# Another order for a planned top-k attention and Mixer: three-piece output products, new priorities, earlier release of score buffers

## The chip, the cores and the metric

The kernel runs on one core of one Trainium2 chip. The metric is the device time of one execution in microseconds (us), as the median of several runs; three runs of the kernel before gave 1004.16, 1005.12 and 1007.36 us.

## What is computed

For 8 batches and 8 heads, with 576 positions and a head dimension of 64: scores are formed, only the 32 largest of each row are kept, and their softmax weights the values. The heads are joined to x (576 x 512 for each batch), and a Mixer block follows, first over tokens, then over channels.

```python
scores = scale * np.matmul(q, k.transpose(0, 1, 3, 2))
kth = np.partition(scores, -top_k, axis=-1)[..., -top_k:-top_k + 1]      # top_k = 32
scores = np.where(scores >= kth, scores, -1000000000.0)
attn = np.exp(scores - np.max(scores, axis=-1, keepdims=True))
attn = attn / (np.sum(attn, axis=-1, keepdims=True) + 1e-09)
x = np.matmul(attn, v)                     # heads joined: (8, 576, 512)
...
h = np.maximum(x.transpose(0, 2, 1) @ w_tok1, 0.0) @ w_tok2    # 576 -> 256 -> 576
u = x + h.transpose(0, 2, 1)
out = u + np.maximum(u @ w_ch1, 0.0) @ w_ch2                   # 512 -> 1536 -> 512
```

## The kernel before

**Units.** The work is cut into 32 units, each two heads of one batch; four units make a batch, and each batch ends in a Mixer. A unit's score rows are nine tiles of 128 rows: eight whole ones (four row blocks of two heads) and one made of both heads' last 64 rows. Tiles 0 to 3 are the unit's first half (group 0), tiles 4 to 8 the second (group 1).

**The stages of a half unit, and their engines.**

- TensorE transposes q and k (`qk_tr`), ScalarE copies the result out of PSUM (`qk_ev`). TensorE makes the scores (`s1_mm`, `s0_mm` at line 334, `st_mm`), ScalarE copies them into the score buffer SS (`s1_ev`, `s0_ev` at line 344, `st_ev`).
- VectorE selects: `upper` (line 384), `split4` (lines 407 and 411), four `top_round`s (lines 423 and 426), `low_round` (line 432), which needs `both_bits` and `lower_bits` of GpSimd (lines 390 and 399), and `combine` (lines 438 to 443), which writes the thresholds `kthall`. GpSimd keeps four numbers of each row (`keep_ends`, line 449), from which the end of the program sees whether the fast selection was sound.
- For five tiles of a unit (0, 1, 2, 4, 5) GpSimd scales the thresholds (`raise_kth`, line 496, tile `kbig`), ScalarE makes a steep ramp (`steep`, line 502), GpSimd subtracts it from the scores (`sink`, line 510), ScalarE takes the exponential into `pb` (`expo`, line 483), and SyncE starts a DMA that transposes it into PT (`turn`). For the other four, ScalarE makes E (`expo`) and a mask U (`below_act`, line 526), and TensorE transposes both in one accumulation (`p_tr`, `ptail_tr`, lines 532 and 535), which ScalarE copies into PT (`p_ev`, line 555, and `ptail_ev`).
- TensorE multiplies PT with the values (`o_mm`, line 601, one call for each head), VectorE takes reciprocals (`o_den`, line 613), ScalarE scales into Xb (`o_ev`, line 624).

**The Mixer.** After each unit `h1_mm` and `ut_mm` do the token part for 128 channels. After a batch's fourth unit `h2_mm` (line 689; 12 blocks, each in two parts) and `out_mm` (lines 711 to 719) do the channel part. One `out_mm` is 15 products into one PSUM bank: x by an identity matrix, two of the token part, twelve of the channel part; there are five in a batch, one for each row block. The last batch has a path of its own (`plan_mlp_last`).

**What sets the order.** Nothing runs in the order in which it is written. Every step is a task with an engine, a planned duration, a priority (smaller goes first), predecessors, and the buffers that it takes (`acq`) and frees (`rel`). `Plan.order` plays this through: when an engine is free, the ready task with the smallest priority whose buffers are free is next. The result is the order in which instructions stand on each engine; each engine then works strictly in that order and waits where an input is not there. A wrong planned duration costs nothing by itself, but it puts an instruction where it has to wait. For unit u the priorities are U = 100u plus an offset; for batch b's Mixer M = 400(b + 1) plus an offset. The PSUM banks are tp (two), s0 (three, scores), O (one) and mps (two, Mixer); SS has four buffers, two units' worth.

Two rules of the plan matter below. Sinks and `keep_ends` of a half are held until `lower_bits` of the next half is done (`hold`, `later`). And where TensorE has been idle in the plan, `spare` (line 244) puts fillers in: products whose result nobody reads.

At the end of a half a task of no duration on GpSimd frees its buffers, once the last readers and `keep_ends` are done:

```python
add("POOL", 0.0, U - 1000, lambda: None, deps=done + [keep[g]],
    rel=[("SS", u, g), ("A", u, g), ("nmax", u, g)] + ([("St", u)] if g else [])
    + ([] if fast else [("kbig", u, g)]))
```

Of the kernel before, what the change touches and what calls it, by code (L numbers as in the profile page):

```python
# [11 lines left out]
LAG = {"PE": 0.11, "ACT": 0.15, "DVE": 0.12, "POOL": 0.06, "SP": 1.2, "DQ": 0.0, "SPQ": 0.0}  # L12
# [3 lines left out]
SPARE = 0.8  # L16
SPARE_US = 0.22
# [7 lines left out]
class Plan:  # L25
# [23 lines left out]
    def order(self):  # L49
# [10 lines left out]
        while left:  # L60
# [13 lines left out]
            for e in free:  # L74
# [14 lines left out]
                if best is not None:  # L89
                    ready[e].remove(best)  # L90
                    if e == "PE" and best.dur > 0.0:
                        at, r, i = min(
# [4 lines left out]
                        )  # L97
# [30 lines left out]
def kernel(  # L128
# [11 lines left out]
    nc = tc.nc  # L140
# [565 lines left out]
    def out_mm(mst, sc):  # L706
        Xb, H1T, H2T = mst["Xb"], mst["H1T"], mst["H2T"]
        ss = csz(sc)
        ss_ = slice(sc * P, sc * P + ss)
        ps = bank("mps")  # L710
        nc.tensor.matmul(
            out=ps[0:ss, 0:C], lhsT=identB[0:ss, 0:ss], rhs=Xb[0:ss, sc, :], start=True, stop=False
        )
        for jc in range(NJ):
            nc.tensor.matmul(
                out=ps[0:ss, 0:C], lhsT=w2b[:, jc, ss_], rhs=H1T[:, jc, :], start=False, stop=False
            )
        for fc in range(NF):
            nc.tensor.matmul(  # L719
                out=ps[0:ss, 0:C],  # L720
                lhsT=H2T[:, fc, ss_],
                rhs=wc2b[:, fc, :],
                start=False,
                stop=(fc == NF - 1),
            )
        mst["po", sc] = ps
# [91 lines left out]
    def plan_unit(u):  # L818
# [5 lines left out]
        for name, src in (("q", q), ("k", k), ("v", v)):  # L824
            ld[name] = add("SP", 1.75, U - 230, lambda name=name, src=src: load_one(st, name, src, b, p),
                           acq=[("ld" + name, u)])
        vc = add("POOL", 1.2, U - 50, lambda: vcast(st), deps=[ld["v"]], acq=[("vb", u)],
                 rel=[("ldv", u)], slack=1.3)
        ev, prev = [], None
        for i in range(2):  # L830
            a = add("PE", 0.61, U - 160, lambda i=i: qk_tr(st, i), deps=[ld["qk"[i]], prev], acq=[("tp", u, "q", i)] + ([] if i else [("qkT", u)]), slack=1.3)
            prev = a
            ev.append(
                add("ACT", 0.49, U - 150, lambda i=i: qk_ev(st, i), deps=[a] + ev[-1:],
                    rel=[("tp", u, "q", i)])
            )
        a = add("PE", 0.29, U - 160, lambda: qk_tail_tr(st), deps=[prev], acq=[("tp", u, "t")])
        add("PE", 0.0, U - 160, lambda: None, deps=[a], rel=[("ldq", u), ("ldk", u)])
        ev.append(
            add("ACT", 0.17, U - 150, lambda: qk_tail_ev(st), deps=[a] + ev, rel=[("tp", u, "t")])  # L840
# [6 lines left out]
        for g in range(2):  # L847
            a = add("PE", 0.65, U - 140 + 10 * g, lambda g=g: s1_mm(st, g), deps=ev + smm[-1:],
# [3 lines left out]
            for hh in range(2):  # L852
                evs.append(
                    add("ACT", 0.17, U - 130 + 10 * g, lambda g=g, hh=hh: s1_ev(st, g, hh), deps=[a] + evs,
# [3 lines left out]
            for t in (2 * g, 2 * g + 1):  # L858
                a = add("PE", 1.1, U - 140 + 10 * g + 1, lambda t=t: s0_mm(st, t), deps=[smm[-1]],
                        acq=[("s0", u, t, 0), ("s0", u, t, 1)])  # L860
                smm.append(a)
                for hh in range(2):
                    evs.append(
                        add("ACT", 0.495, U - 130 + 10 * g + 1, lambda t=t, hh=hh: s0_ev(st, t, hh),
                            deps=[a, e0], rel=[("s0", u, t, hh)])
                    )
            if g == 1:
                for part in range(2):
                    a = add("PE", (1.01, 0.28)[part], U - 129, lambda part=part: st_mm(st, part),
# [4 lines left out]
                        add("ACT", (0.49, 0.12)[part], U - 119, lambda part=part: st_ev(st, part),  # L874
# [5 lines left out]
            x = add("DVE", (2.33, 3.19)[g], U + 5 * g, lambda g=g: split4(st, g), deps=[x, chain.get("low")])  # L880
# [16 lines left out]
            x = add("DVE", (1.33, 1.13)[g], U + 5 * g, lambda g=g: combine(st, g, u), deps=[x])  # L897
            keep_ = add("POOL", 0.25, U + 5, lambda g=g: keep_ends(st, g, u), deps=[x])
# [3 lines left out]
            for i in gtiles(g):  # L902
                if i not in st["turned"]:
                    y = add("ACT", 0.68, U - 50 + i, lambda i=i: expo(st, i), deps=[nm, preE] + evs, acq=[("E", u, i)])
                    selE[i] = preE = y
# [282 lines left out]
```

## Time and profile before

| | us |
|---|---|
| median of three runs | 1005.12 |
| profiled execution, its own time | 1006.08 |
| its span, first to last instruction | 1004.2 |
| TensorE busy (fillers included) | 935.5 |
| VectorE busy | 894.6 |
| ScalarE busy | 853.5 |
| GpSimd busy | 727.9 |
| mean granted TensorE clock, of full speed | 0.979 |

The profile is of one execution. An engine's busy time is the time in which at least one of its instructions runs; what it waits for is in a view of its own. In the timeline a row is one instruction or several alike, with start and length, and in brackets the idle time ahead of it and what ended it. In rows of groups stand count, busy time, mean length of one in ns, and idle time ahead. PE is TensorE, DVE VectorE, ACT ScalarE, POOL GpSimd, SPq the DMA queue of SyncE.

### The profile page before, as it was taken

The numbers are of one execution on the slowest core, as the hardware profiler recorded it, in microseconds if no ns is written. First come the engines' busy times: TensorE is split into PE (matmuls) and PEld (weight loads), VectorE is DVE, ScalarE is ACT, GpSimd is POOL, SyncE is SP. The second block draws the span as 40 slices with busy tenths as digits, with TensorE's granted clock in tenths as the row PEclk, the third lists the DMA queues.
The fourth block names the chain that finished last, engine by engine and source line by source line (L and its number), as shares of the span: only waits on it lengthen the run. The fifth ranks groups of instructions, "written<-read, shape, count | busy, mean of one in ns | idle before, by whom it ended". The sixth has DMA issues, their size and how long they took to land. (4 is left out here: it accounts for less than half of the span.)

```text
span 1004.2 us, 22286 instructions
## 1 busy us (share of the span) xinstructions
PE 935.5 (93%) x7128; PEld 502.9 (50%) x7128; DVE 894.6 (89%) x4088; ACT 853.5 (85%) x1976; POOL 727.9 (72%) x598
## 2 busy tenths in 40 slices
PE   9889999899999999999999999899999999989995
PEld 6444444455555455454545455454545555444542
DVE  3999999997999979999799979999799997999801
ACT  5667898898999988998999989999899989999731
POOL 3888888886688858888598867888688885888400
PEclk9989899999999999999999999999999999999998
DMA  7454122133332233123322333232233333211201
GB/s 167 120 174 130 38 63 60 45 63 105 68 69 51 69 87 87 40 62 77 81 58 60 80 100 79 45 68 74 66 69 63 75 99 68 46 34 31 71 1 51
DMA packets 229741, 72.65 MB, mean 72 GB/s; under 512 B 222128, under 2 KB 222704, under 8 KB 229616
## 3 DMA queue, kind: packets, MB, share of 16 engines
q1 hardware_dynamic: 229616, 71.15, 29.8%
q8 instruction: 58, 0.95, 0.4%
q14 instruction: 67, 0.55, 0.2%
HBM read 35.78 MB, written 9.44 MB: 45 GB/s over the span
## 5 line engine op out<-in xcount | busy, mean ns | idle before, releaser
L390 POOL TENSOR_TENSOR lo<-SS 128x1152 int32<-128x1152 int32 x64 | 168.4, 2632 | 205.4 <-DVE A L423 188.4
L423 DVE MAX8 A<-hx 128x8 f32<-128x72 f32 (+2 forms) x1152 | 263.0, 288 | 0.0
L510 POOL TENSOR_TENSOR SS<-SS,U 128x576 f32<-128x576 f32 x158 | 199.4, 1280 | 0.0
L426 DVE MATCH_REPLACE8 hx<-A,hx 128x72 f32<-128x72 f32 (+1 forms) x864 | 198.3, 237 | 0.0
L399 POOL TENSOR_TENSOR lo<-lo,hi 128x1152 int32<-128x1152 int32 x64 | 188.0, 2937 | 0.0
L344 ACT COPY SS<-s 128x512 f32<-128x512 f32 x256 | 140.3, 594 | 21.3 <-PE s L334 20.8
L334 PE MATMUL s<-qkT 64*128 64x512 f32 x512 | 154.3, 646 | 0.0
L483 ACT ACTIVATE pb<-SS,nmax 128x576 bf16<-128x576 f32 x158 | 123.0, 786 | 22.0 <-POOL SS L510 21.4
L601 PE MATMUL O<-vb,PT 128*128 128x65 bf16 (+3 forms) x1600 | 122.7, 200 | 10.6 <-ACT Xb L624 10.3
L384 DVE TENSOR_TENSOR hi<-SS 128x1152 f32<-128x1152 f32 x64 | 85.9, 1342 | 49.1 <-ACT SS L344 49.1
L689 PE MATMUL mps<-UT,wc1b 128*128 128x512 bf16 (+1 forms) x768 | 120.7, 292 | 7.2 <-ACT H2T L702 5.2
L502 ACT ACTIVATE U<-SS,kbig 128x576 bf16<-128x576 f32 x158 | 117.4, 786 | 10.4 <-POOL kbig L496 10.2
L601 PEld LDWEIGHTS <-PT 128*128 128x128 bf16 (+3 forms) x1600 | 91.8, 100 | 56.6 <-issue 21.2
L432 DVE MAX8 A<-lo 128x8 f32<-128x288 f32 x288 | 108.3, 434 | 0.0
L532 PE MATMUL tp<-identB,E 128*128 128x128 bf16 (+1 forms) x650 | 98.0, 226 | 9.2 <-ACT PT L555 6.6
L535 PE MATMUL tp<-identN,U 128*128 128x128 bf16 (+1 forms) x650 | 95.6, 223 | 1.9 <-ACT U L526 1.9
L719 PE MATMUL mps<-wc2b,H2T 128*128 128x512 bf16 (+1 forms) x420 | 96.4, 379 | 0.0
L702 ACT ACTIVATE H2T<-mps 128x512 bf16<-128x512 f32 (+1 forms) x180 | 73.2, 430 | 23.4 <-PE mps L689 23.0
L532 PEld LDWEIGHTS <-E 128*128 128x128 bf16 (+1 forms) x650 | 63.9, 101 | 48.1 <-issue 37.5
L689 PEld LDWEIGHTS <-wc1b 128*128 128x128 bf16 x768 | 49.8, 99 | 75.5 <-issue 43.8
L244 PEld LDWEIGHTS <-identB 128*128 128x128 bf16 x650 | 56.5, 103 | 59.0 <-issue 14.8
L624 ACT ACTIVATE Xb<-O,rden 128x64 bf16<-128x64 f32 (+1 forms) x320 | 70.8, 319 | 17.7 <-DVE rden L614 17.3
(100 smaller groups left out, 1760.0 us busy)
## 6 DMA issues: line engine op xcount, KB each, us to landing
qL<-in_q_dram SPq DMA_DIRECT2D x64, 128.0 KB, 2.5
kL<-in_k_dram SPq DMA_DIRECT2D x64, 128.0 KB, 2.5
vL<-in_v_dram SPq DMA_DIRECT2D x64, 128.0 KB, 2.5
out_dram<-ob SPq DMA_DIRECT2D x32, 256.0 KB, 2.1
wst<-in_moe_w_ch_dram SPq DMA_DIRECT2D x4, 1536.0 KB, 7.1
PT<-pb SPq DMA_TRANSPOSE x158, 2.4
qL<-in_q_dram SPq DMA_DIRECT2D x32, 32.0 KB, 2.4
kL<-in_k_dram SPq DMA_DIRECT2D x32, 32.0 KB, 2.3
```

Of the source, the lines that this page charges most:

```text
L334: nc.tensor.matmul(out=x[:, :], lhsT=T[rows[hh], 0, t * P : (t + 1) * P], rhs=T[rows[hh], 1, 0:W], start=True, stop=True,)
L344: nc.scalar.copy(out=st["SS", t // 2][:, 2 * (t % 2) + hh, 0:W], in_=st["s0", t][hh][:, :])
L390: nc.gpsimd.tensor_tensor(out=x[:, at, :].bitcast(i32), in0=left.bitcast(i32), in1=right.bitcast(i32), op=ALU.add,)
L399: nc.gpsimd.tensor_tensor(out=x, in0=x, in1=st["hi"][:, 0:n, :].bitcast(i32), op=ALU.subtract)
L423: nc.vector.max(A[:, i, 8 * r : 8 * r + 8], hx[:, i, 0:w])
L426: nc.vector.match_replace(hx[:, i, 0:w], A[:, i, 8 * r : 8 * r + 8], hx[:, i, 0:w], NEG)
L483: nc.scalar.activation(out=x, in_=srow(st, i), func=AF.Exp, bias=st["nmax", g][:, a : a + 1], scale=scale,)
L502: nc.scalar.activation(out=U[:, :], in_=srow(st, i), func=AF.Relu, bias=st["kbig", g][:, a : a + 1], scale=-STEEP,)
L510: nc.gpsimd.tensor_tensor(out=x, in0=x, in1=st["U", i][:, :], op=ALU.subtract)
L532: nc.tensor.matmul(out=out, lhsT=st["E", i][:, cols], rhs=identB[:, :], start=True, stop=False)
L601: nc.tensor.matmul(out=O[0:ms, t, :], lhsT=PT[0:kz, hh, j, t * P : t * P + ms], rhs=st["vb"][0:kz, j, hh, :], start=(j == 0), stop=(j == N ...
L689: nc.tensor.matmul(out=ps[:, 0 : hi - lo], lhsT=wc1b[:, cc, fc * P : (fc + 1) * P], rhs=mst["UT"][:, cc, lo:hi], start=(cc == 0), stop=(cc ...
```

## The change

- `out_mm` is planned and issued in three tasks of five products each, one after the other into the same bank; the bank is taken by the first and given back after the copy that follows the third.
- All priorities of the steps named above come from a table, `RANK`, with new numbers. Scores' products go from U - 140 to U - 161, their copies from U - 130 to U - 136, the output products from M + 260 to M + 275, loads from U - 230 to U - 170, `steep` keeps U - 20, sinks go from U to U + 120.
- Score buffers, St, nmax and kbig are freed in the plan by a task on an engine of its own, which is never busy, as soon as the last readers are done; A is freed after `keep_ends`. No instruction belongs to these tasks.
- Planned durations: `vcast` 1.2 to 0.85, `split4` (2.33, 3.19) to (2.35, 2.8), `combine` (1.33, 1.13) to (1.49, 1.17), `keep_ends` 0.25 to 0.4, `raise_kth` 0.25 to 1.3, `sink` 1.32 to 1.25.
- The search for a bank for fillers allows that none is free.

```diff
+PARTS = 3
+RANK = {
+    "load": -170, "vcast": 25, "qk_tr": -160, "qk_ev": -174, "s_mm": -161, "s_ev": -136, "st_mm": -129, "st_ev": -140,
+    ...
-    def out_mm(mst, sc):
+    def out_mm(mst, sc, part):
...
+        if part == 0:
+            mst["po", sc] = bank("mps")
+        ps = mst["po", sc]
+        terms = [(identB[0:ss, 0:ss], Xb[0:ss, sc, :])]
+        terms += [(w2b[:, jc, ss_], H1T[:, jc, :]) for jc in range(NJ)]
+        terms += [(H2T[:, fc, ss_], wc2b[:, fc, :]) for fc in range(NF)]
+        n = len(terms)
+        for x in range(part * n // PARTS, (part + 1) * n // PARTS):
             nc.tensor.matmul(
+                out=ps[0:ss, 0:C], lhsT=terms[x][0], rhs=terms[x][1],
+                start=(x == 0), stop=(x == n - 1),
             )
...
-                a = add("PE", 1.1, U - 140 + 10 * g + 1, lambda t=t: s0_mm(st, t), deps=[smm[-1]],
+                a = add("PE", 1.1, U + RANK["s_mm"] + 10 * g + 1, lambda t=t: s0_mm(st, t), deps=[smm[-1]],
...
-                        kb = add("POOL", 0.25, U - 1100, lambda g=g: raise_kth(st, g), deps=[kd[g]], acq=[("kbig", u, g)])
+                        kb = add("POOL", 1.3, U - 1100, lambda g=g: raise_kth(st, g), deps=[kd[g]], acq=[("kbig", u, g)])
...
-            add("POOL", 0.0, U - 1000, lambda: None, deps=done + [keep[g]],
-                rel=[("SS", u, g), ("A", u, g), ("nmax", u, g)] + ([("St", u)] if g else [])
+            add("FREE", 0.0, 0, lambda: None, deps=done, slack=0.0,
+                rel=[("SS", u, g), ("nmax", u, g)] + ([("St", u)] if g else [])
                 + ([] if fast else [("kbig", u, g)]))
+            add("FREE", 0.0, 0, lambda: None, deps=[keep[g]], rel=[("A", u, g)])
...
-            a = add("PE", 3.38, M + 260 + 30 * sc, lambda sc=sc: out_mm(mst, sc), deps=hs + oms, acq=[("mps", b, "o", sc)],
-                    rel=[("H2T", b), ("H1T", b), ("Xb", b)] if sc == NS - 1 else [])
-            oms.append(a)
+            for part in range(PARTS):
+                done = sc == NS - 1 and part == PARTS - 1
+                a = add("PE", 3.38 / PARTS, M + RANK["out_mm"] + 30 * sc, lambda sc=sc, part=part: out_mm(mst, sc, part),
+                        deps=hs + oms[-1:], acq=[] if part else [("mps", b, "o", sc)],
+                        rel=[("H2T", b), ("H1T", b), ("Xb", b)] if done else [])
+                oms.append(a)
```

Eight lines are added near the top, so that a line 344 of the kernel before is line 352 after.

How this moves instructions, at two places. The first is ScalarE at the score copies of unit 8, the first unit whose selection meets a Mixer's end. `U<-SS,kbig` is `steep` (two of them in a row belong to a unit's second half, three to its first), `SS<-s` with 128x512 is `s0_ev` (four in a half), with 128x2x64 `s1_ev`, `Xb<-O` is `o_ev`, `pb<-SS,nmax` the exponential of a tile that was sunk, `PT<-tp` are `p_ev` and `ptail_ev`, `UT` is `ut_ev`. Before:

```order
L324 COPY SS<-s_148 128x2x64
L324 COPY SS<-s_149 128x2x64
L502 ACTIVATE U<-SS,kbig 128x576 x2
L344 COPY SS<-s_147 128x512
L344 COPY SS<-s_148 128x512
L624 ACTIVATE Xb<-O_150,rden 128x64 x4
L624 ACTIVATE Xb<-O_150,rden 64x64
L344 COPY SS<-s_149 128x512
L344 COPY SS<-s_147 128x512
```

After:

```order
L491 ACTIVATE pb_134<-SS,nmax 128x576
L563 ACTIVATE PT<-tp_146 128x4x128
L563 ACTIVATE PT<-tp_145 128x4x128
L352 COPY SS<-s_147 128x512
L691 CAST UT<-mps_151 128x512
L567 ACTIVATE PT<-tp_146 128x4x2x64
L583 ACTIVATE PT<-tp_145 64x2x128
L691 CAST UT<-mps_152 128x64
L596 ACTIVATE PT<-tp_146 64x2x64
L332 COPY SS<-s_148 128x2x64
L332 COPY SS<-s_149 128x2x64
L510 ACTIVATE U<-SS,kbig 128x576 x3
```

All four copies of unit 8's first half stood behind the `steep`s of unit 7's second half; now the last of them (the `COPY SS<-s_147` of the second fence) stands ahead of the `steep`s of unit 7's first half.

The second is GpSimd between `lower_bits` of a second half (`lo<-lo,hi` with 1440 columns) and `both_bits` of the next first half (`lo<-SS`). `SS<-SS,U` are the sinks, `ends<-A` is `keep_ends`, `kbig` `raise_kth`. Before:

```order
L399 TENSOR_TENSOR lo<-lo,hi 128x1440
L510 TENSOR_TENSOR SS<-SS,U 128x576 x3
L496 TENSOR_SCALAR kbig<-kthall 128x5
L449 COPY ends<-A 128x16
L390 TENSOR_TENSOR lo<-SS 128x1152
```

After:

```order
L407 TENSOR_TENSOR lo<-lo,hi 128x1440
L457 COPY ends<-A 128x16
L518 TENSOR_TENSOR SS<-SS,U 128x576 x3
L504 TENSOR_SCALAR kbig<-kthall 128x5
L398 TENSOR_TENSOR lo<-SS 128x1152
```

`keep_ends` has moved ahead of the sinks; the rest stands as it stood.

## Rows read from the trace of the kernel before

**Rows 1.** The page's first part: busy time of each engine.

```profile
PE 935.5 (93%) x7128; PEld 502.9 (50%) x7128; DVE 894.6 (89%) x4088; ACT 853.5 (85%) x1976; POOL 727.9 (72%) x598
```

**Rows 2.** Waits of VectorE, 20 to 930 us: total, times, longest.

```profile
DVE hi L384 <- ACT SS L344: 33.9, 6, 6.5
DVE rden L613 <- PE O L601: 1.4, 2, 1.1
```

**Rows 3.** Timeline of VectorE: start, length, instruction, idle time ahead.

```profile
252.27 1.36 DVE L384 TENSOR_TENSOR hi<-SS 128x1152 f32<-128x1152 f32 x1 [5.06 <-ACT SS L344]
...
279.93 1.33 DVE L384 TENSOR_TENSOR hi<-SS 128x1152 f32<-128x1152 f32 x1
...
307.55 1.33 DVE L384 TENSOR_TENSOR hi<-SS 128x1152 f32<-128x1152 f32 x1
...
943.53 0.28 DVE L443 TENSOR_SCALAR kthall<-K 128x5 f32<-128x5 f32 x1
```

**Rows 4.** Timeline of TensorE ahead of the first wait.

```profile
242.09 2.75 PE L719 MATMUL mps<-wc2b,H2T 128*64 128x512 bf16 x12
...
249.84 1.14 PE L334 MATMUL s<-qkT 64*128 64x512 f32 x4
```

**Rows 5.** Timeline of ScalarE in the first wait.

```profile
247.88 1.45 ACT L502 ACTIVATE U<-SS,kbig 128x576 bf16<-128x576 f32 x2
...
251.16 1.08 ACT L344 COPY SS<-s 128x512 f32<-128x512 f32 x2
```

**Rows 6.** Timeline of GpSimd in the first wait, and in unit 9.

```profile
245.93 0.24 POOL L496 TENSOR_SCALAR kbig<-kthall 128x5 f32<-128x5 f32 x1
...
290.25 0.21 POOL L449 COPY ends<-A 128x20 f32<-128x20 f32 x1
290.42 1.27 POOL L510 TENSOR_TENSOR SS<-SS,U 128x576 f32<-128x576 f32 x1
```

**Rows 7.** Groups of ScalarE: count, busy us, mean ns, idle ahead.

```profile
L344 ACT COPY SS<-s 128x512 f32<-128x512 f32 x256 | 140.3, 594 | 21.3 <-PE s L334 20.8
L483 ACT ACTIVATE pb<-SS,nmax 128x576 bf16<-128x576 f32 x158 | 123.0, 786 | 22.0 <-POOL SS L510 21.4
...
L555 ACT ACTIVATE PT<-tp 128x512 bf16<-128x512 f32 x98 | 57.5, 610 | 2.5 <-PE tp L535 2.5
```

**Rows 8.** Fillers (line 244) over the span: products, weight loads, clock, DMA.

```profile
0.00:1004.20 1004.20, 149.58 (x650) 56.53 (x650) 0.98 0.30 72
```

**Rows 9.** Busy PE, PEld, DVE, ACT, POOL: 124 to 930, and six waits.

```profile
124.00:930.00 806.00, 763.34 (x5926) 410.93 (x5924) 763.24 (x3555) 737.68 (x1725) 624.88 (x504) 0.99 0.29 67
...
sum 64.00, PE 63.75 PEld 35.53 DVE 28.65 ACT 62.30 POOL 8.70; mean PE 10.63 PEld 5.92 DVE 4.78 ACT 10.38 POOL 1.45
```

**Rows 10.** Group of `raise_kth`; waits of ScalarE and GpSimd, 20 to 930 us.

```profile
L496 POOL TENSOR_SCALAR kbig<-kthall 128x4 f32<-128x4 f32 x32 | 39.8, 1245 | 4.5 <-DVE kthall L443 0.8
...
ACT U L502 <- POOL kbig L496: 10.2, 20, 1.0
...
POOL lo L390 <- DVE A L423: 185.3, 57, 15.9
```

**Rows 11.** Groups of VectorE: line 438 by shape.

```profile
L438 DVE TENSOR_SCALAR X<-A 128x92 f32<-128x92 f32 x32 | 22.6, 706 | 1.1
...
L438 DVE TENSOR_SCALAR X<-A 128x115 f32<-128x115 f32 x32 | 8.7, 272 | 1.0
```

**Rows 12.** DMA issues: the largest load of the token weights, us to landing.

```profile
wst<-in_moe_w_tok_dram SPq DMA_DIRECT2D x1, 576.0 KB, 5.8
```

**Rows 13.** Busy time and granted clock (PEclk) where TensorE was idle early.

```profile
45.00:50.00 5.00, 1.37 (x14) 1.37 (x14) 5.00 (x11) 4.37 (x10) 4.17 (x3) 0.78 0.22 45
50.00:55.00 5.00, 5.00 (x25) 2.40 (x23) 5.00 (x35) 3.34 (x7) 5.00 (x4) 0.54 0.78 306
```

**Rows 14.** Timelines: one attention product on TensorE, its reciprocals on VectorE.

```profile
266.62 1.90 PE L601 MATMUL O<-vb,PT 128*128 128x65 bf16 x25
...
272.45 0.17 DVE L613 RECIPROCAL rden<-O 128x4 f32<-128x4 f32 x1
```

More of the change, by code (lines that the diff above doesn't have):

```diff
@@ L16 @@
 SPARE = 0.8
+PARTS = 3
+RANK = {
+    "load": -170, "vcast": 25, "qk_tr": -160, "qk_ev": -174, "s_mm": -161, "s_ev": -136, "st_mm": -129, "st_ev": -140,
+    "keep": 5, "exp_u": -56, "steep": -20, "sink": 120, "exp_t": -66, "below": -20, "p_tr": 90, "p_ev": 20,
+    "pt_tr": 65, "pt_ev": 24, "o_mm": 50, "o_ev": 90, "h1_mm": 0, "h1_ev": -40, "ut_mm": 121, "ut_ev": -9,
+    "out_mm": 275, "out_ev": 185, "h2_mm": 40, "h2_ev": -60,
+}
 SPARE_US = 0.22
@@ L91, in order @@
                     if e == "PE" and best.dur > 0.0:
-                        at, r, i = min(
+                        idle = [
                             (max(freed[r][i], free[e]), r, i)
@@ L96, in order @@
                             if slots[r][i] is None
-                        )
+                        ]
+                        at, r, i = min(idle) if idle else (now, "", 0)
                         n = int((now - at) * SPARE / SPARE_US)
@@ L868, in plan_unit @@
                 for part in range(2):
-                    a = add("PE", (1.01, 0.28)[part], U - 129, lambda part=part: st_mm(st, part),
+                    a = add("PE", (1.01, 0.28)[part], U + RANK["st_mm"], lambda part=part: st_mm(st, part),
                             deps=[smm[-1]], acq=[("s0", u, "st", part)],
@@ L873, in plan_unit @@
                     evs.append(
-                        add("ACT", (0.49, 0.12)[part], U - 119, lambda part=part: st_ev(st, part),
+                        add("ACT", (0.49, 0.12)[part], U + RANK["st_ev"], lambda part=part: st_ev(st, part),
                             deps=[a] + ([evs[-1]] if part else []),
@@ L896, in plan_unit @@
             chain["low"] = x
-            x = add("DVE", (1.33, 1.13)[g], U + 5 * g, lambda g=g: combine(st, g, u), deps=[x])
-            keep_ = add("POOL", 0.25, U + 5, lambda g=g: keep_ends(st, g, u), deps=[x])
+            x = add("DVE", (1.49, 1.17)[g], U + 5 * g, lambda g=g: combine(st, g, u), deps=[x])
+            keep_ = add("POOL", 0.4, U + RANK["keep"], lambda g=g: keep_ends(st, g, u), deps=[x])
             kd[g] = x
@@ L920, in plan_unit @@
                     if i % 4 == 0:
[L921 to L922 removed]
+                        kb = add("POOL", 1.3, U - 1100, lambda g=g: raise_kth(st, g), deps=[kd[g]], acq=[("kbig", u, g)])
+                    m = add("ACT", 0.68, U + RANK["steep"] + i, lambda i=i: steep(st, i), deps=[kb, chain.get("steep")], acq=[("U", u, i)])
                     chain["steep"] = m
[L924 removed]
+                    x = add("POOL", 1.25, U + RANK["sink"] + i, lambda i=i: sink(st, i), deps=[m, chain.get("sink")], rel=[("U", u, i)])
                     chain["sink"] = x
                     hold[g].append(x)
[L927 removed]
+                    y = add("ACT", 0.68, U + RANK["exp_t"] + i, lambda i=i: expo(st, i), deps=[x, nmx[g], chain.get("pexp")], acq=[("P", u, i)])
                     chain["pexp"] = y
@@ L995, in plan_mlp @@
             for part in range(2):
-                a = add("PE", (0.97, 0.24)[part], M + 70 + 15 * fc, lambda fc=fc, part=part: h2_mm(mst, fc, part),
+                a = add("PE", (0.97, 0.24)[part], M + RANK["h2_mm"] + 15 * fc, lambda fc=fc, part=part: h2_mm(mst, fc, part),
                         deps=mst["ute"] + wl, acq=[("mps", b, "h2", fc, part)],
@@ L1154 @@
             for sc in range(NS):
-                out_mm(mst, sc)
+                for part in range(PARTS):
+                    out_mm(mst, sc, part)
                 out_ev(mst, sc)
```

68 lines of the change are left out of this document (25 added, 43 removed).

## The prediction

> **What bounds the kernel now.** Read first the page's busy times: VectorE is busy 894.6 of 1004.2 us, ScalarE 853.5, TensorE 935.5 [rows 1]. TensorE's figure is not its need: the fillers that the planner puts into idle TensorE time are in it. Then the waits of VectorE between 20 and 930 us: apart from 1.4 us it waits for one thing only, the copies of scores out of PSUM (line 344), six times, 33.9 us in all [rows 2]. So VectorE, which does the top-32 selection, sets the pace, and everything else is late only in those six places. The timeline of VectorE says where [rows 3]: one unit (two heads) of selection takes 307.55 - 279.93 = 27.62 us, and the wait stands before the first `upper` of a unit: 5.06 us at 252.27. Five more repeat it, 28.8 us together; counted from the start the six stand before units 8, 12, 16, 20, 24 and 28. Those are the units in which the selection meets a Mixer's end.
>
> Why there: on TensorE five output products of the Mixer, each with twelve products of 2.75 us in its tail, stand ahead of the scores; the last ends at 242.09 + 2.75 = 244.84, the scores that VectorE needs begin to be made at 249.84 [rows 4]. On ScalarE the order is worse: two `steep` instructions at 247.88, which need the thresholds of unit 7's second half, stand ahead of the copies of unit 8's first half, the last of which starts at 251.16 [rows 5]. VectorE thus finishes unit 7 and then waits for a chain that could not begin before it finished: `raise_kth` at 245.93 [rows 6], steep, scores, copies, selection.
>
> **The change part by part.** *Order of score copies.* This is the term that counts. In the new order I looked, for each half unit, at the last score copy on ScalarE and at the latest selection whose thresholds an instruction ahead of it needs. Before: in units 8, 12, 16, 20, 24, 28, and nowhere else, that is the selection directly ahead, so that a wait is built in. After: it is never the one directly ahead; at least a whole half unit lies between, in most units two. The first order fence shows it: the last copy of unit 8's first half now stands ahead of `steep` of unit 7's first half. What remains ahead of it and depends on VectorE are two exponentials of unit 6, whose `sink` follows unit 7's `lower_bits`. In the trace the second such sink ends at 290.42 + 1.27, which is 11.8 us after its unit's start [rows 3, 6]. Behind it the new order puts the second exponential, two PT copies and the score copy: 0.79 + 2 x 0.61 + 0.59 = 2.6 us [rows 7]. So the scores are there 14.4 us into a unit of 27.6 us: a margin of 13 us where there was a deficit of 5. All six waits should go: **-33.9 us**.
>
> *Output products in three pieces.* The same 525 products of seven Mixers in the same banks; nothing is added. The twelve last products of a whole one take 2.75 us [rows 4], 0.23 each; a piece of five takes 1.2 us, a whole one 3.4, so a score product waits less behind it. An output bank is held longer, and the first and second products of the next unit need a bank of the same two. I price that at nothing, covered by the margin of 13 us; without it, it would cost at most one piece, 1.2 us, in each of 35 products: 42 us of TensorE time, against 149.6 us of fillers that do no work [rows 8] (650 of them; 543 in the new order).
>
> *Can ScalarE pay?* Between 124 and 930 us ScalarE is busy 737.7 of 806 us [rows 9]. Without the 33.9 us it must do this in 772.1: 95.5%; 34.4 us of its 68.3 idle us may stay. In the six stretches around the waits it is busy 62.3 of 64 us [rows 9], so its idle time lies elsewhere, and half of that must go. Part of it is of the planner's making: `raise_kth` was planned at 0.25 us and takes 1.245, and ScalarE waits 10.2 us for it, twenty times [rows 10]; with 1.3 in the plan another instruction is put there. The rest should shrink when ScalarE runs behind, since its inputs then wait for it. I leave 2 us in the sum for what VectorE will still wait.
>
> *Score buffers freed by the last reader; durations.* Neither adds an instruction; both only move rows. On GpSimd `keep_ends` now stands ahead of the sinks (second order fence). It takes 0.21 us there [rows 6], and the next `both_bits` waits for VectorE 57 times as it is, 185.3 us in all [rows 10], so nothing of it comes on the path. One term is unknown: line 438 of VectorE takes 706 ns in the first half and 272 in the second, though it is the smaller there [rows 11]; 0.43 x 32 = 13.9 us of VectorE time depend on what GpSimd runs beside it. At best all of it goes (-13.9); at worst each waits for a whole sink of 1.27 us [rows 6], (1.27 - 0.43) x 32 = +27. I take 0: between `lower_bits` and the end of the second sink stand the same three instructions before and after. The Trainium skill (SBUF — State Buffer, "Who interferes with whom") says that VectorE in its two-port mode and GpSimd share a port pair that whoever starts first holds for a whole instruction; the trace agrees with this (706 against 272 ns), and by that rule too the sum stays as it is, unless the sinks come later, where it would be a gain of up to 13.9 us.
>
> *Loads and the clock.* The queries of unit 2 now stand behind the first weights, the largest of which lands after 5.8 us [rows 12], and unit 2's transposes stand ahead of unit 1's scores. These are needed a whole unit, 27.6 us, after the first; that covers it. Without the cover it costs 5.8 us once. Later loads only move on SyncE's queue, among the transposing DMAs, with a whole unit of lead. TensorE's clock fell to 0.78 and then 0.54 after a stretch in which the engine was busy 1.37 of 5 us [rows 13]. The Trainium skill (TensorE: Matmul & The Clock Gate, "What's actually happening") has the half rate as the default that activity lifts; it speaks against fewer fillers. The rows bear it out at that place, but the span that has to be filled shrinks too, and a stretch of 5 us at half rate costs 2.5 us of TensorE time under a margin of 13 us: 0 in the sum.
>
> *The end.* VectorE's last threshold is done at 943.53 + 0.28 = 943.8 [rows 3], 60.4 us before the span ends at 1004.2. The rows behind it (attention of unit 31, last Mixer) stand in the same order but for unit 30's UT products: +-1.3 us, taken as 0.
>
> **The sum.** Profiled execution 1006.08 - 33.9 + 2 = 974.2 us. That execution was 0.96 us above the median of 1005.12, so the forecast is 973.2, say 973.5.
>
> **Rivals.** *ScalarE becomes the bound.* It keeps three quarters of the 66.6 us that it idles outside the six stretches (50 us): 737.7 + 50 = 787.7 instead of 806, a gain of 18.3, 986.8 us. For it: 95.5% is much for an engine that works in order; against it: margins of 13 us let it run behind without VectorE noticing.
>
> *The waits only move* (the change does not do what its order promises): ScalarE keeps all 66.6 us, VectorE waits in smaller pieces at other units, 1005 us. Against it: no wait of VectorE outside the six places.
>
> *Slower: VectorE waits for the attention output.* Each half of a unit's attention ends in reciprocals on VectorE, 64 pairs, placed by the plan. In the trace they start 272.45 - (266.62 + 1.90) = 3.9 us after the product is complete [rows 14]. If ScalarE, now with less slack, delivers PT so late that each product comes 4.7 us later against VectorE's order, VectorE waits 0.8 us in each of 62 pairs: 50 us, and 1006.1 - 33.9 + 50 - 1 = 1021. It decides from 4.5 us of lateness on (62 x 0.55 = 34). Against it: now these waits come to 1.4 us [rows 2].
>
> **How the numbers follow.** Forecast 0.70, ScalarE as the bound 0.19, waits that move 0.05, slower 0.06. The forecast's own range is 966 (a few us of line 438 as well) to 981. The range 966 to 991 takes in the first rival and leaves about 0.13 out. About 0.3% (3 us) is what a measurement can tell from no change: faster 0.89, same 0.05, slower 0.06.
>
> **What would show it.** Right: no wait for line 352 (344 before) on VectorE after the first; ScalarE above 94% between 124 and 900 us; VectorE's last threshold near 910. Wrong: waits of VectorE for score copies spread over many units (first rival), or for the O bank at the reciprocals (last rival), or an end more than 63 us after the last threshold.

## The result

Four runs of the changed kernel gave 973.03 to 974.46 us, median 973.64; four of the kernel before beside them had a median of 1006.13. The ratio is 0.9679, with a 95% interval of 0.9659 to 0.9699. The forecast was 973.5.

### The profile page after: what moved, and what is told of

It is laid out like the page before. It is cut to its first block, busy times and chain, and to the rows that moved or that the text cites. A ratio compares the mean times of both kernels' runs of the same rounds, so it can differ in the third digit from the quotient of the medians.

```text
span 971.5 us, 22080 instructions
## 1 busy us (share of the span) xinstructions
PE 909.8 (94%) x7021; PEld 493.5 (51%) x7021; DVE 896.0 (92%) x4088; ACT 850.4 (88%) x1976; POOL 718.6 (74%) x598
## 5 line engine op out<-in xcount | busy, mean ns | idle before, releaser
L342 PE MATMUL s<-qkT 64*128 64x512 f32 x512 | 163.0, 658 | 2.2 <-ACT SS L332 2.2
L352 ACT COPY SS<-s 128x512 f32<-128x512 f32 x256 | 143.5, 597 | 15.0 <-PE s L342 14.8
L697 PE MATMUL mps<-UT,wc1b 128*128 128x512 bf16 (+1 forms) x768 | 113.2, 287 | 9.9 <-ACT H2T L710 9.1
L540 PE MATMUL tp<-identB,E 128*128 128x128 bf16 (+1 forms) x650 | 95.9, 223 | 8.3 <-ACT PT L567 3.9
L726 PE MATMUL mps<-wc2b,H2T 128*128 128x512 bf16 (+1 forms) x420 | 102.2, 380 | 0.0
L392 DVE TENSOR_TENSOR hi<-SS 128x1152 f32<-128x1152 f32 x64 | 86.1, 1345 | 14.3 <-ACT SS L352 14.3
L697 PEld LDWEIGHTS <-wc1b 128*128 128x128 bf16 x768 | 53.6, 97 | 85.0 <-issue 41.7
L710 ACT ACTIVATE H2T<-mps 128x512 bf16<-128x512 f32 (+1 forms) x180 | 69.8, 432 | 23.1 <-PE mps L697 22.8
L491 ACT ACTIVATE E<-SS,nmax 128x576 bf16<-128x576 f32 x98 | 73.7, 780 | 17.7 <-POOL nmax L477 17.2
L504 POOL TENSOR_SCALAR kbig<-kthall 128x4 f32<-128x4 f32 (+1 forms) x63 | 79.5, 1262 | 8.3 <-DVE kthall L451 1.2
```

What stands on the lines that cost most here:

```text
L342: nc.tensor.matmul(out=x[:, :], lhsT=T[rows[hh], 0, t * P : (t + 1) * P], rhs=T[rows[hh], 1, 0:W], start=True, stop=True,)
L352: nc.scalar.copy(out=st["SS", t // 2][:, 2 * (t % 2) + hh, 0:W], in_=st["s0", t][hh][:, :])
L491: nc.scalar.activation(out=x, in_=srow(st, i), func=AF.Exp, bias=st["nmax", g][:, a : a + 1], scale=scale,)
L540: nc.tensor.matmul(out=out, lhsT=st["E", i][:, cols], rhs=identB[:, :], start=True, stop=False)
L697: nc.tensor.matmul(out=ps[:, 0 : hi - lo], lhsT=wc1b[:, cc, fc * P : (fc + 1) * P], rhs=mst["UT"][:, cc, lo:hi], start=(cc == 0), stop=(cc ...
```

## The profile after

Lines are eight higher than before: the score copy is line 352, `upper` 392, `combine` 446 to 451, `steep` 510. The profiled execution took 973.35 us, its span is 971.5. The page's busy times, to be held against [rows 1]:

```profile
PE 909.8 (94%) x7021; PEld 493.5 (51%) x7021; DVE 896.0 (92%) x4088; ACT 850.4 (88%) x1976; POOL 718.6 (74%) x598
```

VectorE has the same work in 33 us less. TensorE is busy 26 us less, while its fillers alone fell by 30 (149.6 us [rows 8] to 119.4). The longest waits of VectorE over the whole span (total, times, longest):

```profile
DVE H2T L1052 <- PE mps L697: 30.0, 12, 5.2
DVE hi L392 <- ACT SS L352: 14.3, 1, 14.3
DVE rden L621 <- PE O L609: 8.4, 2, 5.2
```

The one wait for scores left is the first of all, before anything can be selected; the twelve for the last Mixer and the two for attention output lie in the tail, the time after the last threshold. Between 20 and 900 us VectorE waits for nothing, where six waits of 33.9 us stood [rows 2]. Its timeline at units 7 and 8, and its last threshold (start, length, instruction):

```profile
218.84 1.34 DVE L392 TENSOR_TENSOR hi<-SS 128x1152 f32<-128x1152 f32 x1
...
246.45 1.34 DVE L392 TENSOR_TENSOR hi<-SS 128x1152 f32<-128x1152 f32 x1
...
908.77 0.40 DVE L451 TENSOR_SCALAR kthall<-K 128x5 f32<-128x5 f32 x1
```

Unit 8 starts 27.61 us after unit 7 with no idle time ahead, where 5.06 us stood [rows 3]. ScalarE at the same place:

```profile
232.82 0.61 ACT L352 COPY SS<-s 128x512 f32<-128x512 f32 x1
...
235.24 2.12 ACT L510 ACTIVATE U<-SS,kbig 128x576 bf16<-128x576 f32 x3
```

The last score copy of unit 8's first half ends at 233.43, 14.6 us into unit 7 and 13.0 us before it is needed. ScalarE between 124 us and the end of the selection (busy PE, PEld, DVE, ACT, POOL), and its waits for sinks and for `raise_kth` between 20 and 900 us:

```profile
124.00:897.00 773.00, 737.75 (x5841) 404.14 (x5840) 765.50 (x3557) 739.99 (x1739) 617.14 (x504) 0.99 0.32 70
```

```profile
ACT pb L491 <- POOL SS L518: 18.1, 34, 1.9
...
ACT U L510 <- POOL kbig L504: 2.5, 6, 0.9
```

It is busy 740.0 of 773 us, 95.7%, and its wait for `raise_kth` fell from 10.2 us [rows 10] to 2.5.

**The account.** From the first selection to the last threshold VectorE takes 894.8 us (14.35 to 909.17), 33.8 less than the 928.6 before. Inside that stretch its waits for scores (33.9 us) and for attention output (1.4) are gone, and its busy time rose by 1.4 us, from 884.7 to 886.1. The start came 0.8 us sooner, the tail is 1.9 longer (62.3 against 60.4): -33.8 - 0.8 + 1.9 = -32.7, the difference of the spans.

## Experiments: which part did it

Three theories. A: the priorities alone, and of them the contest between attention's transposes (`p_tr`) and those of q and k (`qk_tr`) for the two tp banks. B: the pieces of the output products are what lets score copies through. C: the scores' own priorities do it. All ratios are against the kernel before, run beside each on the same chip. An edit of a priority is shown as the line of the kernel that it amounts to; in the runs it is a number of `RANK`, or of the same table filled with the old numbers.

**New priorities alone**, on the kernel before: whole products, old release, old durations.

```diff
-            a = add("PE", 0.61, U - 160, lambda i=i: qk_tr(st, i), ...
+            a = add("PE", 0.61, U + RANK["qk_tr"], lambda i=i: qk_tr(st, i), ...
... (and so for every step of the table)
```

> The kernel before with the new priorities and nothing else: output products whole, buffers freed as before, old planned durations. Theory A (the priorities decide where the score copies stand, and that is the whole gain): in this order no last score copy stands behind steep of the half unit directly ahead, the smallest margin summed as in the forecast is 8 us, so VectorE has no wait for score copies after the first; 971 to 980 us. Theory B (the pieces are needed, since a whole output product of 3.4 us stands in the way of the scores): waits of some us come back after each Mixer; 990 to 1005 us.

Measured: 974.8 us, ratio 0.9673 (0.9633 to 0.9713), no wait for scores after the first. That is the changed kernel's time. Pieces, release and durations add nothing that can be measured once the priorities are there.

**The changed kernel with the old priorities.**

```diff
-    "load": -170, "vcast": 25, "qk_tr": -160, "qk_ev": -174, "s_mm": -161, "s_ev": -136, ...
+    "load": -230, "vcast": -50, "qk_tr": -160, "qk_ev": -150, "s_mm": -140, "s_ev": -130, ...
```

> The changed kernel with the priorities of the kernel before; pieces, release of buffers and durations stay new. Theory A: in this order the margin of the first half is -3.6 us in units 11, 15, 19, 23, 27 and 31 and at least 1.1 elsewhere, so six waits of about 3.6 us come back, in the units named and not in those of the kernel before: 973.6 + 22 = 995, range 988 to 1002. Theory B (the pieces carry the gain): 971 to 980 us, no waits.

Measured: 996.12 us, ratio 0.9884 (0.9843 to 0.9925). Waits of VectorE between 20 and 900 us:

```profile
DVE hi L392 <- ACT SS L352: 20.1, 5, 4.1
```

Waits of about 4 us are back, five of them and a sixth behind 900, in units 11, 15, 19, 23, 27 and 31, as forecast from the order. They are not the waits of the kernel before, which stood in units 8, 12, 16, 20, 24 and 28. So the whole gain needs the new priorities, as A has it; which contest makes these other waits was not looked into.

**One number**: on the kernel before, attention's transposes go from U to U + 90.

```diff
-                tr = add("PE", 0.58, U + i, lambda i=i: p_tr(st, i), deps=[m, selE[i]], acq=[("tp", u, i)])
+                tr = add("PE", 0.58, U + 90 + i, lambda i=i: p_tr(st, i), deps=[m, selE[i]], acq=[("tp", u, i)])
```

> The kernel before with one number changed: the priority of p_tr, the attention transposes, goes from U to U + 90. Theory A, narrowed: in the kernel before the transposes of k for the unit after a Mixer (U - 160) were held up because the attention transposes of two units ahead (U - 200 by the same count) went first on the two tp banks, and so they and the scores came to stand behind the output products. With this one number they stand ahead of the first output product; the smallest margins are 0.7 to 3 us, so some waits of 1 to 2 us may be left: 972 to 984 us. Theory C (the scores' own priorities moved them): nothing changes, 1003 to 1009 us.

Measured: 973.25 us, ratio 0.9655 (0.9615 to 0.9696): the whole gain from one number.

**Scores' priorities alone** (`qk_tr`, `qk_ev`, `s_mm`, `s_ev`, `st_mm`, `st_ev` new, all others old).

```diff
-                a = add("PE", 1.1, U - 140 + 10 * g + 1, lambda t=t: s0_mm(st, t), deps=[smm[-1]],
+                a = add("PE", 1.1, U - 161 + 10 * g + 1, lambda t=t: s0_mm(st, t), deps=[smm[-1]],
```

> The kernel before with the new priorities of the score side alone (qk_tr, qk_ev, s_mm, s_ev, st_mm, st_ev), that is score products 21 and copies 6 steps earlier. Theory A, narrowed: the transposes of k still stand behind the output products; margins of -4 to -7 us in units 8, 16, 20 and 28 and -1 to -3 in some others, in all about -30: 999 to 1007 us. Theory C: 971 to 985 us.

Measured: 1000.26 us, ratio 0.9933 (0.9912 to 0.9954), with eight waits for scores of 26.8 us in all:

```profile
DVE hi L392 <- ACT SS L352: 26.8, 8, 5.8
```

C falls, for these priorities gave 6 us of 33: a score product cannot be early when its k is late.

That is what the trace shows when one looks for unit 8's transposes on TensorE. The kernel before, then one number, then scores alone:

```profile
205.23 0.63 PE L281 MATMUL tp<-identF,qL 128*128 128x128 f32 x4
...
240.72 0.66 PE L281 MATMUL tp<-identF,kL 128*128 128x128 f32 x4
```

```profile
214.14 0.65 PE L289 MATMUL tp<-identF,qL 128*128 128x128 f32 x4
215.82 0.63 PE L289 MATMUL tp<-identF,kL 128*128 128x128 f32 x4
```

```profile
203.16 0.63 PE L289 MATMUL tp<-identF,qL 128*128 128x128 f32 x4
...
238.67 0.66 PE L289 MATMUL tp<-identF,kL 128*128 128x128 f32 x4
```

Before, k is transposed 35.5 us after q, behind the Mixer's first four output products; with the one number 1.7 us after it, ahead of all of them. In the plan unit 8's transposes have priority 800 - 160 = 640, attention's of unit 6 had 600 and a few more: these took the second tp bank first, and by the time it was free the Mixer's products stood in the row. With U + 90 unit 6's have 690 and more. The trace of the kernel before shows how long the two banks were gone. Attention's transposes on TensorE (and a filler), then their copies on ScalarE:

```profile
210.50 0.22 PE L532 MATMUL tp<-identB,E 128*128 128x128 bf16 x1
...
213.94 0.24 PE L532 MATMUL tp<-identB,E 128*64 128x128 bf16 x1
...
226.87 1.24 PE L244 MATMUL O<-w1b,identB 128*128 128x512 bf16 x5
```

```profile
228.40 0.65 ACT L555 ACTIVATE PT<-tp 128x512 bf16<-128x512 f32 x1
228.88 0.32 ACT L584 ACTIVATE PT<-tp 64x128 bf16<-64x128 f32 x1
```

From 213.94 to 228.4 both banks hold results that ScalarE has not yet copied, and nothing else is written to a tp bank. TensorE had time for fillers at 226.87, so it was the bank that k lacked and not the engine. No run gave the plan a third bank.

**The other side of the contest**: on the kernel before, q and k go ahead of 600 instead (U - 210 = 590).

```diff
-            a = add("PE", 0.61, U - 160, lambda i=i: qk_tr(st, i), ...
+            a = add("PE", 0.61, U - 210, lambda i=i: qk_tr(st, i), ...
```

> The kernel before with one other number changed: the priority of qk_tr, the transposes of q and k, from U - 160 to U - 210, so that they outrank the attention transposes of two units ahead, whose priority (U) stays. If the contest for the two tp banks is the cause, this cures it as p_tr did: the transposes of k stand ahead of the first output product, the smallest margin is 2.8 us, no waits: 971 to 978 us. If p_tr worked in another way (by letting the Mixer's products go first, say), the waits stay: 995 to 1008 us.

Measured: 977.12 us, ratio 0.9707 (0.9687 to 0.9726), no wait for scores after the first. Either number that turns the contest round removes the waits; this settles the place. Here the last threshold is even sooner than in the changed kernel (905.7 us against 909.2), but the tail is 68.1 us long.

**All new priorities but attention's** (`p_tr`, `p_ev`, `pt_tr`, `pt_ev`, `o_mm`, `o_ev` stay old).

```diff
+    ... "p_tr": 0, "p_ev": 20, "pt_tr": 5, "pt_ev": 30, "o_mm": 50, "o_ev": 30, ...
```

> The kernel before with the new priorities except the six of the attention (p_tr, p_ev, pt_tr, pt_ev, o_mm, o_ev), which stay old. Theory A with margins summed from the order: -3, -3, -6, -7 and -8 us in units 8, 11, 15, 19 and 23 and -11 in unit 27, together about -38: no gain, 1003 to 1013 us, with waits in units 11, 15, 19, 23 and 27 instead of 12, 16, 20, 24 and 28. If the other priorities carry part of the gain by themselves: 975 to 995 us.

Measured: 1016.07 us, ratio 1.0095 (1.0075 to 1.0115), 3 us above the expected range. VectorE between 20 and 900 us:

```profile
DVE hi L392 <- ACT SS L352: 33.2, 8, 7.7
DVE rden L621 <- PE O L609: 7.5, 1, 7.5
```

As A has it, waits for scores of the same sum stay, most of it in units 8, 11, 15, 19, 23 and 27, as forecast from the order; what was not expected is one wait of 7.5 us for attention output at the reciprocals. It is the mechanism of the last rival, once instead of 62 times.

**Pieces alone**, on the kernel before.

```diff
-            a = add("PE", 3.38, M + 260 + 30 * sc, lambda sc=sc: out_mm(mst, sc), ...
+            for part in range(PARTS):
+                a = add("PE", 3.38 / PARTS, M + 260 + 30 * sc, lambda sc=sc, part=part: out_mm(mst, sc, part), ...
```

> The kernel before with the output products in three pieces and nothing else new (old priorities, old release of the score buffers, old durations). Theory A (priorities alone): the k transposes of units 8, 12, ... stand in TensorE's row behind attention's transposes still, only that shorter pieces stand in the same place; six waits of VectorE for scores in the middle of the run are left in some form. The sum from ScalarE's order gives three waits of about 4.4 us where there were six of 5.1 to 6.5: VectorE 20 us shorter, 982 to 992 us. Rival B (the pieces are what lets the score copies through): no waits, 971 to 976 us. Third: the pieces change nothing that VectorE waits for, 1003 to 1009 us.

Measured: 984.8 us, ratio 0.9777 (0.9745 to 0.9809), six waits of 13.4 us. Its waits between 20 and 900 us, and unit 8's k on TensorE:

```profile
DVE hi L392 <- ACT SS L352: 13.4, 6, 3.7
```

```profile
232.06 0.66 PE L289 MATMUL tp<-identF,kL 128*128 128x128 f32 x4
```

So B holds in part: the pieces are a cure of their own, worth three fifths of the wait, and not an addition to the other one. Unit 8's k stands between pieces, 8.7 us sooner than before, and the waits in units 8, 12, 16, 20, 24 and 28 are gone; smaller ones stand in units 11, 14, 19, 22, 27 and 30. The old priorities with pieces, early release and new durations gave 996.12; so release and durations together take back some 11 us under the old priorities. Which of the two does was not separated.

## Experiments: VectorE's hidden stalls

With no wait left, what VectorE still loses lies inside its busy time. Line 438 before is in [rows 11]; line 443 of the kernel before, then the same two lines after (count, busy us, mean ns of one, idle ahead):

```profile
L443 DVE TENSOR_SCALAR kthall<-K 128x5 f32<-128x5 f32 x32 | 9.2, 287 | 1.1
...
L443 DVE TENSOR_SCALAR kthall<-K 128x4 f32<-128x4 f32 x32 | 8.0, 249 | 1.1
```

```profile
L446 DVE TENSOR_SCALAR X<-A 128x92 f32<-128x92 f32 x32 | 19.5, 611 | 1.1
L451 DVE TENSOR_SCALAR kthall<-K 128x5 f32<-128x5 f32 x32 | 15.4, 480 | 1.1
...
L451 DVE TENSOR_SCALAR kthall<-K 128x4 f32<-128x4 f32 x32 | 9.9, 308 | 1.1
L446 DVE TENSOR_SCALAR X<-A 128x115 f32<-128x115 f32 x32 | 8.7, 271 | 0.9
```

**`keep_ends` behind the sinks**, which lets the sinks start sooner.

```diff
-    "keep": 5,
+    "keep": 130,
```

> The changed kernel with one number changed: the priority of keep_ends from U + 5 to U + 130, so that it stands behind the sinks again. In the changed kernel the 5-column form of line 451 takes 480 ns instead of 287, since it meets the end of the third sink, which keep_ends ahead of it puts 0.2 us later; the 92-column form of line 446 (611 ns) waits for the end of the second sink likewise. Theory (VectorE stands still while GpSimd holds something the two share): line 451 goes back to about 290 ns (-6 us in all), line 446 falls by up to 0.2 us (-6): 962 to 968 us. If these lengths have nothing to do with GpSimd: 973 to 974 us.

Measured: 974.32 us, ratio 0.9678 (0.9657 to 0.9698): no gain. Its VectorE:

```profile
L392 DVE TENSOR_TENSOR hi<-SS 128x1152 f32<-128x1152 f32 x64 | 89.3, 1396 | 21.0 <-ACT SS L352 14.3 <-POOL lo L407 6.7
...
L446 DVE TENSOR_SCALAR X<-A 128x92 f32<-128x92 f32 x32 | 16.2, 506 | 1.1
...
L451 DVE TENSOR_SCALAR kthall<-K 128x5 f32<-128x5 f32 x32 | 9.5, 296 | 1.1
```

The forms that were to become shorter did: 32 x (0.105 + 0.184 + 0.056) = 11 us, the last from the form of four (308 to 252). About half of it was given back in the two-input instructions behind them: 3.3 us in line 392 (1345 to 1396 ns, 64 times), 1.4 in line 415 (2.5 more in one form, 1.1 less in another) and 1.4 in line 419. The rest went into one wait of 6.7 us for GpSimd's `lower_bits`, ahead of unit 3 at 104 us, whose cause was not looked into. So this run alone does not show that the stall only moves; the runs with the columns and with the reduction, below, do more.

**Odd columns.** The idea was that an odd number of columns keeps VectorE off the port it shares with GpSimd, since 115 columns never wait and 92 do.

```diff
-        X = mgp.tile([P, NS, NA - 1 - NR], f32, name="X", tag="X")
-        nc.vector.tensor_scalar_mul(X[:, 0:n, :], A[:, 0:n, NR : NA - 1], -1.0)
+        m = NA - 1 - NR
+        X = ...                        # rows of 40 in hx, as in A
+        if n % 2:
+            nc.vector.tensor_scalar_mul(X[:, 0:n, 0:m], A[:, 0:n, NR : NA - 1], -1.0)
+        else:
+            k = (n - 1) * NA + m       # 143 columns in a row
+            nc.vector.tensor_scalar_mul(flat[0][:, 0:k], flat[1][:, NR : NR + k], -1.0)
```

> The changed kernel, same order on all engines, with line 446 of the first half working on 143 neighbouring columns instead of 4 x 23 = 92, into the tile hx, which is free then; the columns between are not read. An odd number of columns like the 115 of the second half, which take 271 ns however GpSimd works. Theory as for keep_late: 611 ns become about 300 although the instruction is larger, and VectorE gains 0.3 us in each of 32 units: 963 to 967 us. If size sets the length: it grows to 0.7 us or more, 974 to 978 us.

Measured: 994.32 us, ratio 0.9887 (0.9861 to 0.9913), 20 us slower than the changed kernel; a miss of both theories:

```profile
L448 DVE TENSOR_SCALAR hx<-A 128x115 f32<-128x115 f32 x32 | 34.8, 1089 | 0.9
L452 DVE TENSOR_SCALAR hx<-A 128x143 f32<-128x143 f32 x32 | 20.5, 639 | 1.1
```

128x143 took 639 ns, and 128x115, which had been 271, now 1089: 32 x 0.82 = 26 us. Line 457's form of five (451 before) gave 6.6 us of that back (480 to 274 ns). Two of the 128x115 in the timeline, with the three sinks beside them:

```profile
220.20 3.76 POOL L524 TENSOR_TENSOR SS<-SS,U 128x576 f32<-128x576 f32 x3
222.59 0.22 DVE L448 TENSOR_SCALAR hx<-A 128x115 f32<-128x115 f32 x1
...
247.81 3.76 POOL L524 TENSOR_TENSOR SS<-SS,U 128x576 f32<-128x576 f32 x3
...
250.32 1.34 DVE L448 TENSOR_SCALAR hx<-A 128x115 f32<-128x115 f32 x1
```

The first begins 2.39 us after its sinks did, just ahead of the change from the second sink to the third, and takes 0.22 us. The second begins 0.12 us later in that pattern and takes 1.34: it ends 0.09 us behind the third sink. Of all 32, eight start 2.35 to 2.41 us behind the first sink's start and take 0.22 to 0.25 us; 22 start 2.49 to 2.52 us behind it and take 1.32 to 1.35; the other two lie among the weight casts before 110 us. So being odd is not what spared the 115 columns. The Trainium skill (VectorE: DVE Perf Modes, "What auto-detection actually checks") gives the condition: one source and the destination in SBUF, their outermost counts both even or equal. By it 5 rows written packed do not take the second port, if a packed output counts as one run of 115 (5 against 115), while 5 against 5, 143 against 143 and 4 against 92 do. All four lengths agree (271 ns against 1089, 639 and 611); that packed rows count as one run is the reading that fits them.

**Columns first.** So 92 columns are read as 23 x 4 and written packed, 23 against 92; the half of five rows stays as it was.

```diff
-        nc.vector.tensor_scalar_mul(X[:, 0:n, :], A[:, 0:n, NR : NA - 1], -1.0)
...
+        if n % 2 == 0:
+            v = X[:, :, :].rearrange("p a c -> p (a c)")[:, 0 : n * (NA - 1 - NR)]
+            v = v.rearrange("p (c a) -> p a c", a=n)
+            nc.vector.tensor_scalar_mul(
+                v.rearrange("p a c -> p c a"),
+                A[:, 0:n, NR : NA - 1].rearrange("p a c -> p c a"),
+                -1.0,
+            )
...
```

> Edit on the changed kernel: for a half of four rows line 446 writes its 92 values column by column (read as 23 x 4, written packed as 92; the half of five rows stays), and MAX8 reads them with that stride. In the changed kernel the 92-column form begins 2.01 us into GpSimd's two sinks and ends 0.06 us behind them (0.57 us), the 115-column form takes 0.27 us in the middle of a sink; in the odd-columns run both forms had input and output of equal outer count (5 and 5, 143 and 143) and both waited. Theory 'form' (a single-input instruction asks for the port it shares with GpSimd where the outer counts of input and output are both even or equal, and not where they differ and one is odd): 5 rows against 115 does not ask, 23 against 92 will not ask either; line 446 at 92 columns falls from 611 to about 270 ns, and VectorE gains at most 32 x 0.3 = 9.6 us, less what line 451 behind it loses to the casts of v that GpSimd runs from 0.45 to 1.3 us after that point (up to 0.33 us, 32 times): 962 to 974 us. Theory 'occupancy' (whatever VectorE writes there while sinks run has to wait for them): 92 columns stay at 550 to 650 ns, 972 to 976 us.

Measured: 971.37 us, ratio 0.9642 (0.9618 to 0.9666). Groups of VectorE:

```profile
L392 DVE TENSOR_TENSOR hi<-SS 128x1152 f32<-128x1152 f32 x64 | 91.2, 1425 | 14.4 <-ACT SS L352 14.4
...
L450 DVE TENSOR_SCALAR X<-A 128x92 f32<-128x92 f32 x32 | 10.1, 314 | 1.1
```

The form no longer waits: each of the 32 takes 0.31 or 0.32 us, though it runs in the middle of a sink. "Form" is right. But of the 9.5 us that it and 1.1 us that line 461 (451 before) give, line 392 takes 5.1 (1345 to 1425 ns) and MAX8 (it finds a row's eight largest), reading with a stride, 2.2; line 415's two larger forms nearly cancel (+2.6, -2.4).

**Thresholds by a reduction** as well.

```diff
-        nc.vector.tensor_scalar_mul(kthall[:, c : c + n], K[:, 0:n, 7], -1.0)
+        nc.vector.tensor_reduce(kthall[:, c : c + n], K[:, 0:n, :], AX.X, ALU.min, negate=True)
```

> As the run before, and line 451 (thresholds, 4 or 5 values) made by a minimum over the eight values of MAX8, negated, in place of a product by -1. In the changed kernel line 451 takes 480 ns in the form of five and 308 in that of four, ending 0.03 us behind a sink or a cast each time, and 170 ns when GpSimd is idle. Theory 'the wait goes': 200 to 250 ns in both forms, 32 x (0.25 + 0.08) = 10 us less on VectorE beside the run before: 952 to 964 us. Theory 'the wait moves on': the next instruction, line 392 (two inputs), starts earlier by as much and waits for the same sink: its mean rises from 1345 to 1450 ns or more, and the time stays within 3 us of the run before.

Measured: 968.1 us, ratio 0.9608 (0.9584 to 0.9632).

```profile
L392 DVE TENSOR_TENSOR hi<-SS 128x1152 f32<-128x1152 f32 x64 | 99.0, 1546 | 14.9 <-ACT SS L352 14.9
...
L461 DVE TENSOR_REDUCE kthall<-K 128x5 f32<-128x40 f32 x32 | 6.3, 196 | 1.1
L461 DVE TENSOR_REDUCE kthall<-K 128x4 f32<-128x32 f32 x32 | 6.0, 187 | 1.1
```

"The wait moves on" is nearer: every reduction takes 0.18 to 0.20 us, 11.9 us less in all, and 7.7 of them are paid again by line 392, whose two inputs lie in SBUF. The time fell by 3.3 us.

**The weight casts to ScalarE** as well, which takes the cause away and does not only move the wait: GpSimd no longer runs the four casts of 2.75 to 3.40 us beside which VectorE stood.

```diff
-            x = add("POOL", dcast, prio, cast, deps=[a], rel=[key], slack=8.0)
+            x = add(eng, dcast, prio, cast, deps=[a], rel=[key], slack=8.0)     # "ACT" for the four channel pieces
```

> The run before (columns read as 23 x 4, thresholds by a negated minimum) and the four casts of the channel weights, 128 x 3072 each, given to ScalarE, with the planner's engine changed accordingly. In the run before they take GpSimd 2.7 to 3.2 us each before 92 us, and four of VectorE's two-input instructions that meet them take 3.30, 3.45, 2.91 and 3.42 us where the same forms take 0.76, 0.90, 1.35 and 1.35 us elsewhere: 8.7 us. ScalarE is busy 77.3 of the 109 us from 15 to 124, so it has 32 us for four casts of some 2.5 to 3.5 us. Theory 'the shared port is the whole of it': VectorE's first 124 us shorten by 6 to 9 us and the time falls to 958 to 964 us. Theory 'given back' (the casts stand ahead of score copies in ScalarE's row and VectorE waits for scores, or the two-input instructions meet the next GpSimd instruction instead): new waits for scores before 124 us or the same lengths, 965 to 972 us.

Measured: 956.67 us, ratio 0.9492 (0.9473 to 0.9510), the shortest time of all. The first such instruction in the run with the reduction, and the same one here:

```profile
43.72 3.23 POOL L794 CAST wc1b<-wst 128x3072 bf16<-128x3072 f32 x1
44.27 3.30 DVE L415 TENSOR_TENSOR hx<-hi 128x576 f32<-128x576 f32 x1
```

```profile
43.59 0.75 DVE L415 TENSOR_TENSOR hx<-hi 128x576 f32<-128x576 f32 x1
```

Its waits for scores, over the whole span:

```profile
DVE hi L392 <- ACT SS L352: 14.2, 1, 14.2
```

VectorE's last threshold is 11.7 us sooner (892.05 against 903.74), more than the 8.7 counted from four instructions: by the groups lines 392, 415 and 419 got 3.6, 6.3 and 1.1 us shorter. The time, 11.4 us less, came out below the 958 to 964 expected. ScalarE does each cast in 2.77 us and VectorE waits for no score because of it.

## Why the prediction was right

**The term that counts, -33.9 us: right**, in size and in reason. All six waits went, and the margin worked out for unit 8, 14.4 us into the unit and 13 us ahead of need, was measured as 14.6 and 13.0. The cause was seen one step too late, though: the prediction named what stood ahead of the score copies on TensorE and ScalarE, and not why it stood there. It was the second tp bank, lost by k's transposes to attention's, and one number of the table's many is enough to turn it. Two rows were read a little off, without effect on the sum: 249.84 is where the last of unit 8's first score products begin, not the first (246.87), and the copies at 251.16 are two.

**Pieces at nothing: right for this kernel**, where the priorities had already done the work, as the run with priorities alone shows. The prediction did not see that the pieces by themselves are worth 22 us: the two cures do not add.

**Can ScalarE pay: right.** 95.5% was asked, 95.7% measured; `raise_kth`'s wait shrank as foreseen. The first rival, ScalarE as the bound, did not come.

**2 us for waits left: nothing was left**, and the 1.4 us of waits for attention output went too. What stood in their place was not foreseen: 1.4 us more busy time of VectorE, and a tail 1.9 us longer, outside the 0 +- 1.3 given, with a start 0.8 us sooner. That these nearly cancel, and the forecast of 973.5 lies within 0.2 us of the median, is luck; the term of -33.9 us is not.

**Line 438 at 0: the sum is nearly right, its reason half.** It looked at one line only. Line 438 (now 446) gained 32 x 0.095 = 3.0 us, line 443 (now 451), which takes the same port, lost 32 x (0.193 + 0.059) = 8.1. That `keep_ends` has moved ahead of the sinks explains the loss: with `keep_ends` put behind them line 451 is at 296 ns again. Line 419 (411 before) gave 3.9 us (526 to 468 ns, 64 times), so that VectorE's busy time in the selection rose by only 1.4. The price "up to 13.9 us of gain" for later or earlier sinks was wrong as a price of time: the runs that took the stall away from these lines found about half of it or more in line 392.

**Loads, clock at 0: right.** VectorE waits for no score between 20 and 900 us, so no load was late enough to reach it; the mean granted clock is 0.979 as before.

**The slower rival** was seen once, with attention's priorities left old (7.5 us at the reciprocals); in the changed kernel such waits are in the tail alone.

## What to carry to other kernels

When the pacing engine waits at regular places, follow the late input back past the busy engines to the step that is late for no reason of work, here a transpose 35 us behind its twin for want of a bank, and turn that one contest before rewriting a whole table. When no waits are left, look for one instruction with two lengths: it stalls inside its busy time, and removing the stall there passes much of it, here half to two thirds, to the next instruction that needs the same port. What paid most was to take the work off the engine that holds the port, where a third engine had room.

## What the runs showed of the hardware

Beside GpSimd's sinks a product of 128x115 with a constant takes 0.27 us or 1.09 on average depending on how its output lies (packed, or in rows as far apart as the input's), with the same count of elements. Where it needs the port, 0.12 us of arrival decides between 0.22 and 1.34 us, since sinks follow one another: one that came just ahead of the change between two sinks ran at once, one that came at the change ended 0.09 us behind the next sink. A two-input instruction (line 415) takes 3.30 us beside a GpSimd cast of 3.23, and 0.75 where the cast is not there. None of this shows as idle time of VectorE. The Trainium skill (SBUF — State Buffer, "Who interferes with whom") has reductions of VectorE on trn2 never contending and instructions with two inputs in SBUF contending with GpSimd's reads; the traces agree with both, 196 against 480 ns for the thresholds and 1546 against 1345 for line 392.
